# Attention at eight steps to a unit in the second tile of tokens, and the sums of the first weights only from the third

## The chip, the cores and the metric

One core of one Trainium2 chip runs the whole program. The metric is device microseconds from the first to the last instruction, as a median over runs; a trace of one profiled execution is used for everything that is read inside.

## What is computed

```python
k_p = k.reshape(B, H, Sp, pool, D).mean(axis=3)      # B, H, S, D = 8, 8, 576, 64; pool = 8
v_p = v.reshape(B, H, Sp, pool, D).mean(axis=3)
scores = scale * np.matmul(q, k_p.transpose(0, 1, 3, 2))
...
attn = attn / (np.sum(attn, axis=-1, keepdims=True) + 1e-09)
return np.matmul(attn, v_p)
...
x = attn_out.transpose(0, 2, 1, 3).reshape(B * S, H * D)     # 4608 x 512
h = x @ w_in;  x = np.maximum(0.01 * h, h) @ w_out           # d_ff = 2048
h = x @ w_in2; r = np.maximum(h, 0.0); out = (r * r) @ w_out2
```

So: attention over keys and values pooled by eight, then two two-layer networks, all in float32. The weights come in as 64-bit numbers, whose two halves the kernel decodes itself.

## The kernel before, in words

Every float32 operand of a large matmul is split into a high and a low part, and three matmuls (lines 274, 275, 276) make one product. The first network handles 3072 of the 4608 tokens plainly, in six tiles of 512 tokens. A tile has 16 units, one for each 128 columns of the hidden layer; unit u of all 96 is tile u // 16. A unit is `first` (12 matmuls into the tile h), an activation and a split on ScalarE and VectorE, and `second` (12 matmuls into the four accumulators acc). The remaining tokens, and the whole second network, are computed afterwards as seven products of half-sized blocks ("the products"), which need sums of weight blocks prepared before.

Three streams of other work are woven into the 96 units:

- **Attention** is a generator of 237 steps that remain after the first batch. It works on 40 chunks of 128 or 64 queries, five to a batch. `stage_a` transposes the queries (trq), `stage_b` makes the scores (s, line 470), the negated maximum (mx, 478), the difference (x, 486, from batch 3 on), the exponential, its sum (491), the reciprocal rs (493) and, on GpSimd, the probabilities p (495, 502). `stage_c` transposes p (pt, 513, and pr, 522) and splits the result (515, 525), and `stage_d` multiplies by the values (o). Up to unit 15 three steps are advanced in each unit, and five in each unit after that: half of them, rounded down, between `first` and `second`, the others behind `second`.
- **Sums of the first weights** (`prepare_sums`, lines 203 to 206, then the split at 219 and 220): 32 steps, sixteen pairs of one sum step and one split step. One step is advanced in each unit once all weights are decoded and the tile number is above 0.
- **Preparation of the second network's weights** (`prepare_products`): 136 steps, three in each unit, once attention has ended and the sums are done.

The tiles trq, trk, s, pt, pr, o and h share one pool of four PSUM buffers (`ps_w`), taken in the order in which the code asks for them. A tile can be written only when the readers of the fourth tile before it are through. The accumulators have the other four.

A scheduler lays the instructions of each engine in an order of its own before the program runs; on the chip each engine then follows its order strictly. So the code's steps set priorities, and independent work, like the sums, is drawn ahead of its place in the code.

Of the kernel before, what the change touches and what calls it, by code (L numbers as in the profile page):

```python
# [33 lines left out]
def attention_two_mlps(  # L34
# [22 lines left out]
    SPANS = (320, 256)  # L57
    EARLY = 3
    AHEAD = 5
    RATES = (3, 5)  # L60
    HT = 384
    NTILE = 6
    NPASS = NT // (2 * HT)
# [60 lines left out]
    def tick(n=1):  # L124

        for one in LATE:
            one[0] -= n
        while LATE and LATE[0][0] <= 0:
            nc.sync.dma_start(**LATE.pop(0)[1])
# [52 lines left out]
    def split_weights(kind, t, f):  # L182

        w = W[kind, f]
        hl = hlpool.tile([P, 2, TT], F32R, tag="hl", name=f"hl_{kind}_{t}_{f}")
        hi, lo = hl[:, 0], hl[:, 1]
        nc.scalar.copy(hi, w)
        nc.vector.tensor_tensor(out=lo, in0=w, in1=raw(hi), op=ALU.subtract)  # L188
        HL[kind, t, f] = (hi, lo)
        if t == NTILE - 2:  # L190
            p, i = f % NQ, f // NQ
            for j in range(2):
                part = {(0, 0): 0, (0, 1): 1, (1, 1): 2}.get((i, j) if kind == "in" else (j, i))
                if part is not None:
                    later(
                        2, out=WD[1, kind, p // 2][part, :, p % 2].rearrange("p (h x) -> p h x", h=2),
                        in_=raw(hl)[:, :, j * HD:(j + 1) * HD],
                    )
# [408 lines left out]
    def put_stores(until):  # L607

        while STORES and STORES[0][0] <= until:
            nc.sync.dma_start(**STORES.pop(0)[1])  # L610
# [10 lines left out]
    def load_x(t):  # L621
        XS[t] = []
        for c in range(NK):
            st = temp(f"xs1_{t}_{c}")
            nc.sync.dma_start(out=st, in_=x0[t][c * P:(c + 1) * P, :])
            XS[t].append(st)

    def split_x(t):
        new_x(t)
        for (hi, lo), st in zip(X[1, t], XS.pop(t)):  # L630
            nc.scalar.copy(hi, st)
            nc.vector.tensor_tensor(out=lo, in0=st, in1=raw(hi), op=ALU.subtract)
# [4 lines left out]
    def first(t, f):  # L637

        x = X[1, t]
        wh, wl = HL.pop(("in", t, f))  # L640
        h = work(f"h1_{t}_{f}")
        for c in range(NK):
            cs = slice(c * P, (c + 1) * P)
            three(h, (wh[:, cs], wl[:, cs]), x[c], c == 0, c == NK - 1)
        g = temp(f"g1_{t}_{f}")
        nc.scalar.activation(g, h, AF.Prelu, alpha=0.01)
        gh = gpool.tile([P, TT], F32R, tag="gh", name=f"gh1_{t}_{f}")
        gl = gpool.tile([P, TT], F32R, tag="gl", name=f"gl1_{t}_{f}")
        nc.scalar.copy(gh, g)  # L649
        nc.vector.tensor_tensor(out=gl, in0=g, in1=raw(gh), op=ALU.subtract)  # L650
        G[t, f] = (gh, gl)
# [12 lines left out]
    def second(t, f):  # L664
        gh, gl = G.pop((t, f))
        wh, wl = HL.pop(("out", t, f))
        if f == 0:
            A[t] = [ps_a.tile([P, TT], F32, tag="acc", name=f"acc1_{t}_{j}") for j in range(4)]
        acc = A[t]
        for j in range(4):  # L670
            js = slice(j * P, (j + 1) * P)
            three(acc[j], (wh[:, js], wl[:, js]), (gh, gl), f == 0, f == NF - 1)
        if f == NF - 1:
            for j in range(4):
                o = temp(f"o1_{t}_{j}")
                if j % 2 == 0:
                    nc.scalar.copy(o, acc[j])
                else:
                    nc.vector.tensor_copy(o, acc[j])
                store_x1(t, j, o)  # L680
# [6 lines left out]
    def load_x2(t):  # L687
        XS2[t] = []
        for j in range(2):
            src = x0[NTILE + 2 * t + j] if t < LEAD else x1[2 * (t - LEAD) + j]  # L690
            st = x2pool.tile([P, NK, HT], F32, tag=f"xs{j}", name=f"xs2_{t}_{j}")
            nc.sync.dma_start(out=st, in_=src.rearrange("(c p) n -> p c n", p=P))
            XS2[t].append(st)
# [177 lines left out]
    def prepare_weights(f):  # L871
        if f not in RAW:
            RAW[f] = fetch_weights(1, [("in", f), ("out", f)])
        decode_weights(f)
# [21 lines left out]
    def advance():  # L896
        nonlocal at_work, made
        made += 1
        if next(att, 1):
            at_work = False  # L900
        put_stores(made - 2 if at_work else made)
# [6 lines left out]
    for i, (t, f) in enumerate(units):  # L908
        if f == NF - 3 and t + 1 < NTILE:
            while ready[0] * S < min((t + 2) * TT, NT):  # L910
                advance()
            put_stores(made)
            load_x(t + 1)
        if f == NF - 1 and t + 1 < NTILE:
            split_x(t + 1)

        rate = RATES[min(t, 1)]
        if i + 1 < len(units):
            first(*units[i + 1])
        tick()  # L920
        if i + 2 < len(units):
            split_weights("in", *units[i + 2])
        if i + 1 < len(units):
            split_weights("out", *units[i + 1])
        while at_work and made < due + rate // 2:
            advance()
        second(t, f)
        tick()
        due += rate
        while at_work and made < due:  # L930
            advance()
        if w1 < NF:
            prepare_weights(w1)
            w1 += 1
        elif t > 0:
            next(sums1, None)
        if not at_work:
            if prep is None:
                ppool = ctx.enter_context(tc.tile_pool(name="prep", bufs=1, side="right", reuse_waits="tile"))
                prep = prepare_products()  # L940
            for _ in range(3):
                if preparing and next(sums1, 1) and next(prep, 1):
                    preparing = False
        if t == NTILE - 1 and f >= NQ:
            if x2pool is None:
                assert not at_work and next(sums1, 1)
                w_early_stack.close()
                x2pool = ctx.enter_context(tc.tile_pool(name="x2", bufs=1, side="right", reuse_waits="tile"))
                ring = ctx.enter_context(tc.tile_pool(name="ring", bufs=RING, side="right", reuse_waits="tile"))
                load_x2(0)  # L950
                tick(9)
                blocks.insert(0, next_block())
            else:
                if not XO:
                    xg = products_x(0)
                next(xg, None)
# [47 lines left out]
```

## Time and profile before

| what | value |
|---|---|
| median of three runs | 1665.25 us (1664.63 to 1666.43) |
| the profiled execution's own time | 1667.88 us |
| its span, first to last instruction | 1666.1 us |
| TensorE matmul busy | 1615.4 us, 97% |
| VectorE busy | 1219.9 us, 73% |
| ScalarE busy | 858.3 us, 52% |
| GpSimd busy | 132.5 us, 8% |

A busy share is an average over the whole span. The attention stretch and the products have different limits, so each has to be read from windows of its own. TensorE, VectorE, ScalarE and GpSimd are PE, DVE, ACT and POOL in the profile. In the trace the first h matmuls of units 16, 32, 48, 64 and 80 start at 176.80, 311.14, 440.71, 544.30 and 631.34 us, and attention ends in unit 53, just before 488.82 us.

### The profile page before, as it was taken

Reading aid. Unit: us, or ns where it says so; the run is one execution under the profiler, and the core shown is the slowest. Engines: PE = TensorE matmul, PEld = TensorE weight load, DVE = VectorE, ACT = ScalarE, POOL = GpSimd, SP = SyncE. Lnnn points to the kernel's source line nnn. Section 1 sums busy time; section 2 is a strip of 40 time slices with the busy share of each in tenths; the row PEclk is TensorE's granted clock in tenths of the full one; section 3 lists DMA queues with packets and bytes.
Section 4 is the critical chain, followed back from the end, with each engine's and each line's share of the span. In section 5 each row is a group of like instructions: output and inputs, shape, how many; then the busy total and the mean of one; then the engine's idle time right before and its main releaser. Section 6 shows DMA issues by size and latency. Waiting matters only on the chain.

```text
span 1666.1 us, 26276 instructions
## 1 busy us (share of the span) xinstructions
PE 1615.4 (97%) x9688; PEld 1496.2 (90%) x9688; DVE 1219.9 (73%) x1795; ACT 858.3 (52%) x1527; POOL 132.5 (8%) x149
## 2 busy tenths in 40 slices
PE   4899999999999999999999999999999999999998
PEld 3677778778888888889999999999999999999998
DVE  5899999998778778967628459378477487485484
ACT  5788766655666666756435325334234244244233
POOL 3132223322210000000000000000000000000000
PEclk7799999999999999999999999999999999999999
DMA  7565666663326987979878878978878879878776
GB/s 179 184 197 173 187 195 201 196 216 85 95 92 228 307 303 242 319 278 311 294 273 286 287 258 272 305 254 286 293 249 297 281 251 302 277 247 272 269 253 203
DMA packets 215808, 403.88 MB, mean 242 GB/s; under 512 B 55424, under 2 KB 119936, under 8 KB 215680
## 3 DMA queue, kind: packets, MB, share of 16 engines
q1 hardware_dynamic: 215680, 402.19, 73.5%
q8 instruction: 78, 1.28, 0.3%
q14 instruction: 50, 0.41, 0.1%
HBM read 314.57 MB, written 85.98 MB: 240 GB/s over the span
## 4 chain that ended last, share of the span: by engine, by line
PE 77%; DVE 14%; ACT 3%; DMA 3%; issue 2%; SPq 1%; POOL 0%; DVEq 0%; ACTq 0%; POOLq 0%
PE acc L276 12%; PE h L274 12%; PE acc L275 12%; PE acc L274 12%; PE h L275 12%; PE h L276 12%; DVE gl L650 1%; DVE hl_out L188 1%; PE s L470 1%; DVE hl_in L188 1%; DVE v L313 1%; DMA st_in_out<-in_moe_w_out_dram 1%; DVE mx L478 1%; ACT x L481 1%; DMA xs<-x 1%
## 5 line engine op out<-in xcount | busy, mean ns | idle before, releaser
L696 ACT CAST oh<-g 128x768 fp32r<-128x768 f32 x224 | 187.2, 836 | 283.8 <-PE acc L275 165.1
L275 PE MATMUL h<-xl,wb_in 128*128 128x384 f32 x896 | 299.3, 334 | 0.0
L274 PE MATMUL h<-xh,wb_in 128*128 128x384 f32 x896 | 299.3, 334 | 0.0
L276 PE MATMUL h<-xh,wb_in 128*128 128x384 f32 x896 | 299.3, 334 | 0.0
L697 DVE TENSOR_TENSOR ol<-g,oh 128x768 fp32r<-128x768 f32 x224 | 213.6, 954 | 102.1 <-ACT oh L696 101.3
L276 PE MATMUL acc<-wb_out,ol 128*128 128x256 f32 x1008 | 282.2, 280 | 0.0
L274 PE MATMUL acc<-wb_out,oh 128*128 128x256 f32 x1008 | 281.2, 279 | 0.0
L275 PE MATMUL acc<-wb_out,oh 128*128 128x256 f32 x1008 | 281.2, 279 | 0.0
L275 PEld LDWEIGHTS acc<-wb_out,oh 128*128 128x128 f32 x1008 | 189.5, 188 | 0.0
L276 PEld LDWEIGHTS acc<-wb_out,ol 128*128 128x128 f32 x1008 | 189.2, 188 | 0.0
L274 PEld LDWEIGHTS acc<-wb_out,oh 128*128 128x128 f32 x1008 | 188.5, 187 | 0.0
L791 DVE TENSOR_TENSOR g<-h,s 128x768 f32<-128x768 f32 x32 | 30.6, 956 | 191.7 <-PE h L276 112.2
L275 PEld LDWEIGHTS h<-xl,wb_in 128*128 128x128 f32 x896 | 168.2, 188 | 0.0
L274 PEld LDWEIGHTS h<-xh,wb_in 128*128 128x128 f32 x896 | 168.2, 188 | 0.0
L276 PEld LDWEIGHTS h<-xh,wb_in 128*128 128x128 f32 x896 | 168.2, 188 | 0.0
L274 PE MATMUL h<-xh,hl_in 128*128 128x512 f32 x384 | 153.4, 400 | 4.4 <-DVE x L486 2.2
L274 PE MATMUL acc<-gh,hl_out 128*128 128x512 f32 x384 | 153.7, 402 | 0.7 <-ACT gh L649 0.7
L275 PE MATMUL acc<-gl,hl_out 128*128 128x512 f32 x384 | 150.8, 393 | 1.3 <-DVE gl L650 1.3
L276 PE MATMUL acc<-gh,hl_out 128*128 128x512 f32 x384 | 150.9, 393 | 1.1 <-DVE hl_out L188 1.1
L276 PE MATMUL h<-xh,hl_in 128*128 128x512 f32 x384 | 150.4, 392 | 0.0
L275 PE MATMUL h<-xl,hl_in 128*128 128x512 f32 x384 | 150.0, 391 | 0.0
L700 DVE TENSOR_TENSOR g<-g,g 128x768 f32<-128x768 f32 x128 | 120.7, 954 | 6.1 <-ACT g L758 4.6
(148 smaller groups left out, 2976.9 us busy)
## 6 DMA issues: line engine op xcount, KB each, us to landing
wb_in<-wd_in SPq DMA_DIRECT2D x224, 512.0 KB, 4.4
wb_out<-wd_out SPq DMA_DIRECT2D x224, 512.0 KB, 4.5
xs<-x SPq DMA_DIRECT2D x16, 768.0 KB, 7.1
out_dram<-o SPq DMA_DIRECT2D x24, 384.0 KB, 3.9
k<-in_k_dram SPq DMA_DIRECT2D x64, 128.0 KB, 2.9
q<-in_q_dram SPq DMA_DIRECT2D x32, 256.0 KB, 4.0
st_in_out<-in_moe_w_in_dram SPq DMA_DIRECT2D x16, 512.0 KB, 4.1
st_in_out<-in_moe_w_out_dram SPq DMA_DIRECT2D x16, 512.0 KB, 5.6
```

Of the source, the lines that this page charges most:

```text
L188: nc.vector.tensor_tensor(out=lo, in0=w, in1=raw(hi), op=ALU.subtract)
L274: nc.tensor.matmul(outp, ah, bh, start=first, stop=False, **kw)
L275: nc.tensor.matmul(outp, ah, bl, start=False, stop=False, **kw)
L276: nc.tensor.matmul(outp, al, bh, start=False, stop=last, **kw)
L313: nc.vector.tensor_tensor(out=dst if n == D else src[:, :, 0:n], in0=src[:, :, 0:n], in1=src[:, :, n:2 * n], op=ALU.add)
L470: nc.tensor.matmul(sc[:n, 2 * m:2 * m + 2].rearrange("p a x -> p (a x)"), qT[:, 2 * e + m, :n], kT[b % 2][:, 2 * e + m].rearrange("p a x - ...
L478: nc.vector.tensor_reduce(out=mx[:n], in_=sc[:n], axis=AX.X, op=ALU.max, negate=True)
L481: nc.scalar.activation(x[:n, 4 * e + h], sc[:n, h], AF.Exp, bias=mx[:n, h], accum_out=sm[:n, 4 * e + h],)
L696: nc.scalar.copy(hi, src)
L697: nc.vector.tensor_tensor(out=lo, in0=src, in1=raw(hi), op=ALU.subtract)
L700: nc.vector.tensor_tensor(out=out_, in0=a, in1=b, op=ALU.subtract)
L791: nc.vector.tensor_tensor(out=g11, in0=v, in1=s1, op=ALU.add)
```

## The change

```diff
-    RATES = (3, 5)
+    RATES = (3, 8, 5)
...
-        rate = RATES[min(t, 1)]
+        rate = RATES[min(t, 2)]
...
         if w1 < NF:
             prepare_weights(w1)
             w1 += 1
-        elif t > 0:
+        elif t > 1:
             next(sums1, None)
         if not at_work:
...
-            for _ in range(3):
+            for _ in range(3 if t > 3 else 1):
                 if preparing and next(sums1, 1) and next(prep, 1):
                     preparing = False
```

In the second tile (units 16 to 31) attention advances eight steps to a unit, four before `second` and four behind it, and the sums wait for the third tile. Attention's 237 steps are then used up in unit 44 and no longer in unit 53. From there on the loop at the end advances one step in a unit up to tile 3, first on the sums that are left and then on the preparation, and three from tile 4 on. The number of instructions for each part is the same.

Two places in the order of instructions are shown. The first is TensorE at one chunk of batch 4 (queries 256 to 319), which lies in the second tile in both kernels. The names are those above with the tile, unit or chunk in them; "..." stands for the other 512-column matmuls of the same unit. Before:

```order
L470 MATMUL s_256_0_3260<-kT_162,qT_256_3092 64x144 x2
L470 MATMUL s_256_1_3266<-kT_162,qT_256_3092 64x144 x2
L274 MATMUL acc_1_0_2029<-gh_1_13_3137,hl_out_13_3144 128x512
...
L276 MATMUL acc_1_3_2032<-gh_1_13_3137,hl_out_13_3144 128x512
L513 MATMUL pt_128_3292<-ident,p_128_3114 128x128 x4
L522 MATMUL pr_128_3299<-ident,p_128_3114 96x128 x2
L455 MATMUL trq_448_3306<-ident,q_448_3248 128x128 x4
L274 MATMUL h_1_15_3316<-xh_1_0_1878,hl_in_15_3242 128x512
...
L470 MATMUL s_320_1_3350<-kT_162,qT_320_3255 128x144 x2
L513 MATMUL pt_256_3364<-ident,p_256_3276 128x64 x4
```

And in the changed kernel:

```order
L470 MATMUL s_256_0_3008<-kT_162,qT_256_2882 64x144 x2
L470 MATMUL s_256_1_3014<-kT_162,qT_256_2882 64x144 x2
L513 MATMUL pt_128_3028<-ident,p_128_2904 128x128 x4
L274 MATMUL acc_1_0_2063<-gh_1_8_2849,hl_out_8_2856 128x512
...
L522 MATMUL pr_128_3047<-ident,p_128_2904 96x128 x2
L455 MATMUL trq_448_3054<-ident,q_448_2996 128x128 x4
L470 MATMUL s_320_0_3064<-kT_162,qT_320_3003 128x144 x2
L470 MATMUL s_320_1_3070<-kT_162,qT_320_3003 128x144 x2
L274 MATMUL acc_1_0_2063<-gh_1_9_2981,hl_out_9_2988 128x512
...
L513 MATMUL pt_256_3084<-ident,p_256_3024 128x64 x4
```

Between the scores s_256 and the transpose pt_256 that needs their probabilities stood 24 matmuls of 512 columns (twelve into acc, twelve into h); now there are 17 (twelve and five, all into acc).

The second place is VectorE at the end of the first tile (s_in and w_0, w_8 are the first sum and its weights, k and rk the keys being pooled, kd their result). One piece of the difference:

```order
-L203 TENSOR_TENSOR s_in_2084<-w_8_1009 128x256
-L204 TENSOR_TENSOR s_in_2084<-w_0_268,w_8_1009 128x256
-L205 TENSOR_TENSOR s_in_2084<-s_in_2084,w_0_268 128x256
 L313 TENSOR_TENSOR rk_1836<-rk_1836 64x128
-L206 TENSOR_TENSOR s_in_2084<-w_0_268,s_in_2084 128x256
-L313 TENSOR_TENSOR rr_2157<-rk_1836 64x64
+L313 TENSOR_TENSOR k_0_1838<-k_0_1838 128x2x256
+L313 TENSOR_TENSOR rr_2140<-rk_1836 64x64
```

and a few rows further on in the changed kernel:

```order
L313 TENSOR_TENSOR kd_2139<-k_0_1838 128x128
L313 TENSOR_TENSOR k_2_1843<-k_2_1843 128x2x128
L203 TENSOR_TENSOR s_in_4064<-w_8_1009 128x256
L313 TENSOR_TENSOR kd_2139<-k_2_1843 128x128
L204 TENSOR_TENSOR s_in_4064<-w_0_268,w_8_1009 128x256
```

The first sums, which the code now asks for in unit 32, were moved by about ten rows only: the scheduler still draws them ahead to unit 14.

## Rows read from the trace of the kernel before

**Rows 1.** The page: busy time by engine, and PE and DVE by slices.
```profile
PE 1615.4 (97%) x9688; PEld 1496.2 (90%) x9688; DVE 1219.9 (73%) x1795; ACT 858.3 (52%) x1527; POOL 132.5 (8%) x149
PE   4899999999999999999999999999999999999998
DVE  5899999998778778967628459378477487485484
```

**Rows 2.** Windows by stage: length, busy of PE, PEld, DVE, ACT, POOL; PEclk, DMA, GB/s.
```profile
176.80:311.14 134.34, 127.86 (x680) 104.82 (x677) 129.04 (x268) 87.34 (x208) 39.47 (x40) 1.00 0.63 196
311.14:440.71 129.57, 127.35 (x683) 106.14 (x682) 110.30 (x218) 76.34 (x158) 33.00 (x40) 1.00 0.47 140
440.71:488.82 48.11, 48.11 (x261) 40.26 (x260) 35.38 (x74) 30.62 (x61) 11.41 (x16) 1.00 0.25 74
544.30:631.34 87.04, 87.04 (x385) 72.07 (x384) 69.31 (x113) 58.77 (x98) 0.00 (x0) 1.00 0.92 312
...
1000.00:1200.00 200.00, 200.00 (x1479) 200.00 (x1478) 131.21 (x147) 79.83 (x99) 0.00 (x0) 1.00 0.84 282
```

**Rows 3.** TensorE's waits, units 16 to 63: total us, times, longest.
```profile
PE h L274 <- DVE x L486: 2.2, 3, 1.1
PE pt L513 <- POOL p L495: 1.6, 2, 1.2
PE h L274 <- DVE pt_l L515: 1.3, 1, 1.3
PE pr L522 <- POOL p L502: 1.0, 3, 0.4
```

**Rows 4.** VectorE in the second tile, by line.
```profile
L220 DVE TENSOR_TENSOR hs_out<-s_out,hs_out 128x1024 fp32r<-128x1024 f32 x6 | 7.6, 1263 | 0.0
L220 DVE TENSOR_TENSOR hs_in<-s_in,hs_in 128x1024 fp32r<-128x1024 f32 x5 | 6.3, 1251 | 1.4 <-ACT hs_in L219 1.4
...
L204 DVE TENSOR_TENSOR s_out<-w 128x256 f32<-128x256 f32 x6 | 3.2, 542 | 0.0
```

**Rows 5.** Timeline, second tile, chunk 256 of batch 4: start, length.
```profile
296.37 1.20 PE L470 MATMUL s<-kT,qT 128*64 128x144 f32 x8
297.97 0.81 DVE L478 TENSOR_REDUCE mx<-s 64x4 f32<-64x288 f32 x2
303.67 0.19 DVE L493 RECIPROCAL rs<-sm 64x8 f32<-64x8 f32 x1
304.03 2.49 POOL L495 TENSOR_TENSOR p<-x,rs 64x512 f32<-64x512 f32 x1 [6.83 <-DVE rs L493]
306.58 0.46 PE L513 MATMUL pt<-ident,p 64*128 64x64 f32 x4 [1.21 <-POOL p L495]
```

**Rows 6.** Timeline, end of the third tile, chunk 256 of batch 6.
```profile
407.64 1.19 PE L470 MATMUL s<-kT,qT 128*64 128x144 f32 x8
...
413.58 1.04 POOL L495 TENSOR_TENSOR p<-x,rs 64x512 f32<-64x512 f32 x1 [4.84 <-DVE rs L493]
...
416.53 0.46 PE L513 MATMUL pt<-ident,p 64*128 64x64 f32 x4
```

**Rows 7.** Timeline, second tile: two PSUM tiles and their last readers.
```profile
300.80 0.38 PE L522 MATMUL pr<-ident,p 128*96 128x128 f32 x2
303.22 0.42 DVE L525 TENSOR_TENSOR pt_r<-pr,pt_r 32x256 fp32r<-32x256 f32 x1
304.23 1.14 PE L470 MATMUL s<-kT,qT 128*128 128x144 f32 x8
...
307.36 0.45 DVE L486 TENSOR_TENSOR x<-s,mx 128x288 f32<-128x288 f32 x1
```

**Rows 8.** GpSimd's p by line: second tile, then units 48 to 53.
```profile
L495 POOL TENSOR_TENSOR p<-x,rs 128x512 f32<-128x512 f32 (+1 forms) x11 | 15.4, 1400 | 72.0 <-DVE rs L493 53.1 <-PE o L276 6.9 <-DVE vd L313 6.1
...
L495 POOL TENSOR_TENSOR p<-x,rs 128x512 f32<-128x512 f32 (+1 forms) x5 | 5.2, 1042 | 32.9 <-DVE rs L493 17.5 <-ACT pt_h L514 7.7 <-PE pr L522 7.7
```

**Rows 9.** Timeline, the last unit's second, before the products.
```profile
719.29 0.50 PE L274 MATMUL acc<-gh,hl_out 128*128 128x512 f32 x1 [0.74 <-ACT gh L649]
720.41 0.50 PE L275 MATMUL acc<-gl,hl_out 128*128 128x512 f32 x1 [0.62 <-DVE gl L650]
```

## Prediction

> **What bounds the kernel now.** I read the page first. TensorE is 97% busy, and of the forty slices VectorE is at nine tenths only in the third to the ninth [rows 1]. So the page's 73% for VectorE hides two regimes, and I cut the span at the units' starts. From 544.30 us on TensorE is busy without a gap: sixteen units take 87.04 us, 5.44 us each, and a window in the products is full as well [rows 2]. Nothing that the change moves into those stretches can make them shorter. In the attention stretch the windows differ. In the second tile TensorE is busy 127.86 of 134.34 us and VectorE 129.04; in the third 127.35 of 129.57 and VectorE 110.30; in units 48 to 53 TensorE has no gap at all [rows 2]. The idle time of TensorE that a better weave could win is therefore 6.48 + 2.22 = 8.70 us, half a per cent of the span.
>
> The waits say what that idle time is. 3.5 us (2.2 + 1.3) are h matmuls that wait until VectorE has read a PSUM tile (x or pt_l), and 2.6 us (1.6 + 1.0) are transposes that wait for the probabilities p from GpSimd [rows 3]. The remaining 2.6 us are spread over small ones. VectorE is late in both large classes, but TensorE's order decides whether its lateness shows.
>
> **TensorE's own work is the same in sum.** The 29 attention steps of units 48 to 53 cost (48.11 - 6 x 5.44) / 29 = 0.53 us of TensorE each, with no idle in them [rows 2]. A step costs that wherever it stands, so moving 48 steps from units 32 to 53 into units 16 to 31 neither adds nor saves: time before and after differ by TensorE's idle time alone.
>
> **VectorE in the second tile.** The sums were to leave it, and mostly they don't: the scheduler draws them ahead, so that of the eleven splits of sums that stood there [rows 4] eight are still in the changed order. Three pairs go, each about 1.25 us of split and four sums of some 0.5 us [rows 4]: 3 x 3.2 = 9.6 us. 48 attention steps come in. What one costs VectorE is bounded by 35.38 us less 18 weight and activation splits of about 0.69 us, over 29 steps, (35.38 - 12.4) / 29 = 0.79 us with the preparation's rows counted in [rows 2]; I take 0.75, an estimate. 129.04 + 36.0 - 9.6 = 155.4 us, against 87.04 + 128 x 0.53 = 154.9 us for TensorE. Before, the two stood at 129.0 and 129.4. So the pair of engines is as evenly full as before, over a stretch a fifth longer. This alone changes little. Behind unit 44 VectorE has sums or preparation at about the density of today's units 54 to 79, which cost TensorE nothing.
>
> **Term 1, the waits for p.** With eight steps in groups of four, the scores of a chunk and the transposes of its p come closer. I counted in both orders the TensorE work between them, 0.227 us for a matmul of 512 columns (5.44 / 24) and about 0.11 us for a small one. In the order before, no chunk of the second tile has less than 7.5 us of cover; in the changed one seven of nineteen have 5.0 to 5.9, on average 5.6. The chunk shown in the order falls from 7.5 to 5.9 us, because 17 large matmuls stand where 24 stood. What must fit under it is the chain mx, x, exponential, sum, rs, p. In the second tile it took 306.52 - 297.57 = 8.95 us, and the transpose waited [rows 5]; at the end of the third tile, without sums, 414.62 - 408.83 = 5.8 us, and it fitted under 7.7 us [rows 6]. Those are the two bounds: seven chunks at 5.8 - 5.6 give 1.4 us, at 8.95 - 5.6 they give 23.5 us. In the long one p alone took 2.49 us, where its mean there is 1.40 [rows 5, 8]; with the mean it would be 7.9 us. VectorE is as full as there, but fewer sums stand inside the chains. I take 7.0 us, between 5.8 and 7.9: 7 x 1.4 = 9.8 us, in the place of 2.6 us now.
>
> The row on p also bears on a rule. In the Trainium skill, "SBUF — State Buffer", section "Who interferes with whom", a VectorE instruction with two inputs in SBUF and a GpSimd instruction that reads SBUF exclude each other for a whole instruction. The trace agrees as far as p goes: 1.40 us in the full second tile, 1.04 us in units 48 to 53 [rows 8]. By that rule a denser weave would push p toward its 2.49 us and term 1 to about 7 x 2.5 = 17.5 us.
>
> **Term 2, the four PSUM buffers.** More attention per unit means more tiles through `ps_w` between two h tiles. A pr tile was free 303.64 - 301.18 = 2.46 us after its last write, an s tile 307.81 - 305.37 = 2.44 us [rows 7]. Counting in the order the TensorE work between the last write of an s, pt or pr tile and the first write of the fourth tile behind it, in units 16 to 43: before, five reuses have less than 2.45 us, and they lack 3.7 us together, which is close to the 3.5 us of h waits that the trace shows [rows 3]. After, sixteen have less, and they lack 9.0 us. The lower bound is no change, 3.5 us, if VectorE runs ahead of TensorE; with readers at 3.0 us instead of 2.45 the same count gives 19 us.
>
> **Term 3, the way into the products.** The last unit's `second` waits 0.74 + 0.62 = 1.36 us for ScalarE and VectorE, which are then full of preparation [rows 9]. In the changed order the preparation's last rows stand before unit 93, so I take this gain whole; its other bound is nothing.
>
> **The sum.** Idle time after: 9.8 + 9.0 + 2.6 = 21.4 us if the waits were independent. They aren't: while TensorE waits for p, the readers of PSUM catch up. I take off half of the smaller, 4.5, which is a choice, and have 16.9 us against 8.7. That is +8.2, less 1.4 for term 3: about +7 us. The profiled execution took 1667.88 us (span 1666.1), 2.6 us above the median of the runs, so the same step on the median gives 1665.25 + 7 = 1672 us.
>
> **Rivals.**
> 1. *Faster.* The short covers don't bite, because TensorE is what VectorE waits for in the changed order: the sums no longer stand between mx and rs, and the chain is as short as in the third tile. Then the waits for p cost 1.4 us, those for PSUM stay under today's 3.5 us, say 2, and with the rest halved to 1.3 the idle is 4.7 us in the place of 8.7: -4.0, with term 3 -5.4, 1660 us. For it: chains of 5.8 us exist [rows 6]. Against it: eight of eleven pairs of sums are still in the tile, and VectorE and TensorE come out level. It is decided by the chain: below about 6.0 us it holds, and with term 2 at today's size break-even with term 3 lies at 6.2 us.
> 2. *The change does little.* The stall is set by how full VectorE and TensorE are against each other, and that ratio is 1.00 before and after. Idle time is then moved from units 32 to 43 into 16 to 31: 1665 us, within 3 us. The third tile speaks for it, where the same weave with VectorE at 110.30 of 129.57 lost only 2.22 us [rows 2]; the counted covers speak against it.
> 3. *Much slower.* VectorE falls behind in the second tile and every short cover pays 8.95 - 5.6: 23.5 + 9.0 + 2.6 - 8.7 - 1.4 = +25 us without overlap, with it +20: 1685 us. The trace holds such a chain [rows 5], but one with a slow p.
>
> **Chances and range.** My forecast, waits that grow by 3 to 15 us, has 0.48; rival 1 has 0.20, rival 2 0.24, rival 3 0.08. About 3.3 us (0.2%) is what a measurement of this kernel tells from no change. Slower: 0.48 + 0.08 = 0.56; same 0.24; faster 0.20. The likeliest case alone spans 1668 to 1680. The range for eight in ten has to take in most of rival 1 and the lower end of rival 3, from 1659 to 1684.
>
> **What would show it.** In the profile after, POOL's last work should end near unit 44, some 40 us before today's 488.82 us (nine units of 5.44 us less, and the added idle time more). In units 16 to 31, TensorE's idle time should rise from 6.48 us to 12 or more, under two names: pt and pr waiting for p, and h, trq or o waiting for reads of x, pt_l or pt_r. The gap before the products should be gone. I am wrong if those two waits do not grow: if the stretch from unit 16 to 63, 367.5 us now, is shorter, then the chain or the readers were faster than I took them. I am also wrong if TensorE idles behind unit 44, since I cost the sums and the preparation there at nothing; their cover is 5.44 us of matmuls in each unit, and every us by which VectorE exceeds it would be paid in full.

## The result, and the profile after

| | before | changed |
|---|---|---|
| median of six runs | 1665.95 us | 1676.10 us (1673.92 to 1678.50) |
| ratio | | 1.0057, 95% interval 1.0047 to 1.0067 |
| the profiled execution | 1667.88 us | 1673.92 us |
| its span | 1666.1 us | 1672.2 us |

The change makes the kernel slower by 10.15 us on the median. The two profiled executions are only 6 us apart, because the one of before is among its longer runs and the one after is the shortest of its six. Where that difference lies is seen below.

The page of the changed kernel, busy time by engine:

```profile
PE 1613.8 (97%) x9688; PEld 1491.7 (89%) x9688; DVE 1220.0 (73%) x1795; ACT 857.2 (51%) x1527; POOL 133.7 (8%) x149
```

Beside [rows 1] the page says almost nothing: nearly the same shares, the same counts. The windows by stage do (units 16 to 31, 32 to 47, 48 to 63 and 64 to 79 of the changed kernel; columns as in [rows 2]).

```profile
173.62:339.10 165.48, 153.72 (x852) 125.92 (x849) 154.35 (x330) 102.83 (x252) 52.26 (x59) 0.99 0.56 168
339.10:465.33 126.23, 121.51 (x636) 100.17 (x635) 114.11 (x219) 80.79 (x158) 30.82 (x36) 1.00 0.55 183
465.33:552.37 87.04, 87.04 (x385) 72.07 (x384) 77.11 (x126) 63.27 (x104) 0.00 (x0) 1.00 0.67 229
552.37:639.41 87.04, 87.04 (x385) 72.07 (x384) 66.46 (x107) 55.55 (x95) 0.00 (x0) 1.00 0.91 306
```

TensorE idles 165.48 - 153.72 = 11.76 us in the second tile and 126.23 - 121.51 = 4.72 us in the third, 16.48 together against 8.70 before. In units 48 to 79 it is full, with the preparation there; no sum is left for them, since the last split of a set of sums starts at 429.8 us. The last work of GpSimd ends at 445.1 us and not near 488, in unit 44.

The same difference by stretches: units 16 to 63 took 367.5 us before and take 378.75; from unit 64 to the end it was 1121.8 and is 1119.8; before unit 16 it was 176.8 and is 173.6. The first two make +9.25 us. The third, -3.2 us, hides part of that. I don't count it to the change, which moved the first sums by about ten rows there: the granted clock at the start was lower in the profiled execution of before, and over all the kernels below this start takes 173.6 to 179.8 us. The first window of before, and behind it that of the changed kernel:

```profile
0.00:62.00 62.00, 30.09 (x131) 25.67 (x132) 42.02 (x83) 35.85 (x124) 20.24 (x30) 0.71 0.66 177
```

```profile
0.00:62.00 62.00, 28.49 (x136) 22.44 (x137) 43.81 (x87) 37.25 (x129) 20.70 (x30) 0.81 0.65 178
```

At 0.71 of the 2.4 GHz level TensorE got through 131 matmuls in 62 us, at 0.81 through 136. So all comparisons below are made from unit 16 on, or on medians.

Behind unit 16 the granted clock differs once more. Before, it is 1.00 in all windows of units 16 to 53 [rows 2]. In the changed kernel it was 0.50 (the 1.2 GHz level) for 3.4 us in unit 17. TensorE had been busy for 2.06 of the 4.73 us before, with two waits of 1.8 and 0.8 us:

```profile
184.00:188.73 4.73, 2.06 (x13) 1.25 (x12) 4.67 (x12) 4.02 (x20) 0.71 (x1) 1.00 0.76 247
188.73:192.14 3.41, 3.41 (x15) 2.73 (x14) 3.17 (x8) 2.64 (x12) 1.56 (x3) 0.50 0.29 67
```

At half the clock these 3.4 us cost 1.7 us at most (an estimate from this row), and they show as busy time, not as idle time.

TensorE's waits in units 16 to 63 of the changed kernel (columns as in [rows 3]):

```profile
PE pt L513 <- POOL p L495: 7.5, 8, 1.7
PE trq L455 <- issue: 2.5, 2, 1.7
PE pr L522 <- ACT x L481: 1.8, 1, 1.8
PE pr L522 <- DVE x L486: 1.1, 1, 1.1
PE trq L455 <- ACT x L481: 0.8, 1, 0.8
PE h L274 <- DVE x L486: 0.7, 1, 0.7
PE o L539 <- DVE pt_r L525: 0.5, 1, 0.5
```

The two names of the forecast are there. Waits for p went from 2.6 us [rows 3] to 7.7 (7.5, and 0.2 for pr).

The second name is waits until a PSUM tile has been read. In the list they are those of pr, trq and h for x, 1.8 + 1.1 + 0.8 + 0.7 = 4.4 us (in batches 0 to 2 x comes from ScalarE, line 481, straight from the scores). The two waits of trq put down to "issue" look like the same thing: each ends about 0.1 us behind a reading of scores by VectorE, and in the order shown trq takes the buffer of the first s tile. One of them:

```profile
230.17 0.44 DVE L486 TENSOR_TENSOR x<-s,mx 64x288 f32<-64x288 f32 x1
...
230.71 0.63 PE L455 MATMUL trq<-ident,q 128*128 128x128 f32 x4 [0.77 <-issue]
```

With them this class is 6.9 us. Before, it was the 3.5 us of h in [rows 3] and two smaller lines, 4.9 us in all. These two stand here, from units 16 to 63 of the kernel before; the third line, like the wait for pt_r above, is another thing, as o waits for its own operand:

```profile
PE pr L522 <- DVE pt_l L515: 0.7, 1, 0.7
PE h L274 <- ACT qT L459: 0.7, 1, 0.7
PE o L539 <- DVE pt_r L525: 1.1, 2, 0.7
```

So most of the added idle time has the name p, 5.1 us, and 2.0 us have the name of PSUM readers.

The timeline of the chunk that the order showed (queries 256 to 319 of batch 4), from its scores to its transpose:

```profile
267.83 1.19 PE L470 MATMUL s<-kT,qT 128*64 128x144 f32 x8
...
269.91 0.45 DVE L478 TENSOR_REDUCE mx<-s 64x4 f32<-64x288 f32 x1
270.39 0.80 DVE L650 TENSOR_TENSOR gl<-g,gh 128x512 fp32r<-128x512 f32 x1
...
270.70 0.66 PE L513 MATMUL pt<-ident,p 128*128 128x128 f32 x4 [1.68 <-POOL p L495]
...
274.81 0.69 DVE L188 TENSOR_TENSOR hl_out<-w,hl_out 128x512 fp32r<-128x512 f32 x1 [0.19 <-ACT hl_out L187]
...
276.06 0.19 DVE L493 RECIPROCAL rs<-sm 64x8 f32<-64x8 f32 x1
...
276.42 1.04 POOL L495 TENSOR_TENSOR p<-x,rs 64x512 f32<-64x512 f32 x1 [4.72 <-DVE rs L493]
...
277.51 0.46 PE L513 MATMUL pt<-ident,p 64*128 64x64 f32 x4 [0.60 <-POOL p L495]
```

The scores end at 269.02, p at 277.46: a chain of 8.44 us. In [rows 5] it was 8.95, with a p of 2.49 us; here p takes 1.04, and the length comes from VectorE, which goes from one row to the next with hardly a gap and has the splits of weights and activations (hl_out, gl) between this chunk's own rows. The cover counted in the order was 5.9 us, so the transpose could have been 2.5 us late. It waited 0.60. Inside the cover stands the transpose of the chunk before, which itself waited 1.68 us, and that time was cover too. Here one chunk's wait paid for a part of the next one's.

### The profile page after: what moved, and what is told of

The parts are those of the page before. It is cut to its first block, busy times and chain, and to the rows that moved or that the text cites. A ratio compares the mean times of both kernels' runs of the same rounds, so it can differ in the third digit from the quotient of the medians.

```text
span 1672.2 us, 26299 instructions
## 1 busy us (share of the span) xinstructions
PE 1613.8 (97%) x9688; PEld 1491.7 (89%) x9688; DVE 1220.0 (73%) x1795; ACT 857.2 (51%) x1527; POOL 133.7 (8%) x149
## 4 chain that ended last, share of the span: by engine, by line
PE 82%; DVE 11%; ACT 3%; issue 2%; DMA 1%; POOL 1%; SPq 0%; DVEq 0%; ACTq 0%; POOLq 0%
PE acc L276 13%; PE h L274 13%; PE acc L275 13%; PE acc L274 13%; PE h L276 13%; PE h L275 13%; PE s L470 1%; ACT x L481 1%; DVE hl_out L188 1%; DVE hl_in L188 1%; DVE w L172 1%; DVE wm L162 1%; DVE mx L478 1%; DVE v L313 1%; DVE gl L650 1%
```

## The experiments

The idle time of TensorE in the second and third tile and the stretches are read from windows at each kernel's own unit starts, as above. The last column is for how long the granted clock was 0.50 in units 16 to 63 of the profiled execution; half of it, at most, is lost. Ratios, and differences of medians in the text, are to runs of the kernel before made together with each experiment (medians of 1665.74 to 1666.53 us).

| kernel | median us | ratio to before (95%) | idle, tiles 2 and 3 | units 16 to 63 | unit 64 to end | us at clock 0.50 |
|---|---|---|---|---|---|---|
| before | 1665.95 | | 6.48 + 2.22 | 367.5 | 1121.8 | 0 |
| changed | 1676.10 | 1.0057 (1.0047 to 1.0067) | 11.76 + 4.72 | 378.8 | 1119.8 | 3.4 |
| 1 rate alone | 1680.40 | 1.0083 (1.0070 to 1.0097) | 12.88 + 5.04 | 382.8 | 1119.8 | 6.8 |
| 2 all but the rate | 1671.08 | 1.0027 (1.0017 to 1.0038) | 7.19 + 3.46 | 371.1 | 1123.1 | 3.4 |
| 3 six steps | 1674.55 | 1.0048 (1.0036 to 1.0061) | 7.70 + 5.23 | 378.0 | 1120.1 | 10.2 |
| 4 changed, later transposes | 1673.20 | 1.0038 (1.0026 to 1.0051) | 9.68 + 4.42 | 375.2 | 1119.8 | 3.4 |
| 5 before, later transposes | 1667.12 | 1.0007 (0.9998 to 1.0016) | 5.69 + 3.39 | 367.9 | 1121.0 | 0 |
| 6 changed, six PSUM buffers | 1682.93 | 1.0096 (1.0083 to 1.0110) | 14.92 + 3.79 | 382.8 | 1119.8 | 13.7 |
| 7 before, six PSUM buffers | 1671.82 | 1.0034 (1.0021 to 1.0047) | 7.40 + 3.32 | 371.0 | 1120.8 | 3.4 |
| 8 changed, both distances | 1675.73 | 1.0051 (1.0034 to 1.0068) | 6.33 + 4.56 | 374.2 | 1121.2 | 10.2 |
| 9 changed, sums behind attention | 1691.62 | 1.0153 (1.0139 to 1.0166) | 7.30 + 0.76 | 370.0 | 1142.1 | 3.4 |
| 10 before, sums behind attention | 1688.97 | 1.0139 (1.0124 to 1.0155) | 2.96 + 0.82 | 362.7 | 1147.0 | 3.4 |
| 11 before, sums behind and on GpSimd | 1765.97 | 1.0603 (1.0587 to 1.0619) | 3.02 + 0.82 | 379.8 | 1210.3 | 17.1 |
| 12 before, part of the sums behind | 1675.04 | 1.0052 (1.0039 to 1.0066) | 5.26 + 0.82 | 364.0 | 1132.2 | 0 |

**1. The rate alone.** The kernel before with

```diff
-    RATES = (3, 5)
+    RATES = (3, 8, 5)
-        rate = RATES[min(t, 1)]
+        rate = RATES[min(t, 2)]
```

> The kernel before with eight steps to a unit in the second tile and nothing else changed: sums from the second tile on, preparation at three steps to a unit. Theory (TensorE waits because less of its own work lies between a chunk's scores and its transposes, and between two uses of a PSUM buffer): in the order, seven covers in the second tile are again between 4.8 and 6 us, and PSUM reuses lack 7.6 us in the place of 5.4 before; about 8 to 10 us slower than before, 1674 to 1676 us. Rival (the sums and the preparation that were pushed behind attention cost it): no change from before, 1666 us.

The rate alone costs 14 us (0.83%), above my range and more than the whole change. So the loss comes from the eight steps, and the rest of the change gives a quarter of it back in their presence.

**2. All but the rate.** The changed kernel with

```diff
-    RATES = (3, 8, 5)
+    RATES = (3, 5)
-        rate = RATES[min(t, 2)]
+        rate = RATES[min(t, 1)]
```

> The changed kernel with five steps to a unit in the second tile: the later sums and the slower preparation alone. Theory: the order keeps covers of 7.5 us in the second tile, PSUM reuses lack 4.5 us as against 5.4 before; same as before within 2 us, 1664 to 1668 us. Rival (sums and preparation): the 10 us of the whole change, 1676 us.

It cost 4.5 us, which is in neither range: at five steps the later sums hurt, at eight they helped. Idle time in the two tiles is 10.65 us for 8.70. The largest wait in units 16 to 63 is for the reader of a PSUM tile, 2.2 us before [rows 3]:

```profile
PE h L274 <- DVE x L486: 3.8, 4, 1.9
```

Why a few sums in other places make x late by 1.6 us more I can't show. A part of the 3.6 us that units 16 to 63 take longer can be the clock, 1.7 us at most. The run says that a new order alone, with the same density, moves this kernel by some us.

**3. Six steps to a unit.** The changed kernel with

```diff
-    RATES = (3, 8, 5)
+    RATES = (3, 6, 5)
```

> The changed kernel with six steps in the place of eight. Theory: the order has one short cover in the second tile (5.7 us) in the place of seven, and PSUM reuses lack 4.7 us as before; 0 to 2 us slower than before, 1666 to 1668 us. Rival (VectorE's work in the second tile sets the time): by the counted rows that work is 134 us, 127 before and 149 in the change, so a third of the 10 us, 1669 to 1670 us.

Missed: the kernel is above both ranges and almost as slow as at eight steps. The waits for p are down, in units 16 to 63 of this kernel, to

```profile
PE pt L513 <- POOL p L495: 5.4, 4, 2.6
```

and idle time in the two tiles is 12.93 us, 4.2 more than before, where eight steps have 7.8 more. The rest that makes it look almost as slow as eight steps is busy time, and the clock was low in three places:

```profile
189.66:193.07 3.41, 3.37 (x12) 2.98 (x12) 3.29 (x7) 2.69 (x10) 2.27 (x3) 0.50 0.30 69
295.47:298.88 3.41, 3.41 (x9) 2.64 (x9) 3.09 (x9) 0.87 (x2) 0.05 (x1) 0.50 0.59 194
408.11:411.52 3.41, 3.41 (x10) 2.64 (x9) 1.32 (x4) 0.66 (x1) 1.35 (x3) 0.50 0.02 5
```

That is up to 5.1 us, against up to 1.7 in the changed kernel. By idle time, one step more costs about half of what three cost.

**4. and 5. Later transposes.** To take the first of the two classes of waits away, `stage_c` of a chunk runs a chunk later from batch 2 on, with three p buffers in the place of two (the room comes from a mask kept as one column and broadcast). The core of it:

```diff
+            LAGGED, c_done = 2 * nch, 0
...
+                behind = 1 if i <= LAGGED else 2
+                for j in range(c_done, len(chunks) if i == len(chunks) else i - behind + 1):
+                    b, span = chunks[j][:2]
+                    yield from stage_c(*chunks[j])
+                    c_done = j + 1
...
                 if i > 0:
-                    b, span = chunks[i - 1][:2]
-                    yield from stage_c(*chunks[i - 1])
...
```

In the changed kernel:

> The changed kernel with p transposed one chunk later from batch 2 on (a third p buffer; the mask is kept as one column, which makes room for it). The arithmetic is the same. Theory: the covers in the second tile are 13.7 us and more, so the waits of pt and pr for p, 7.5 us of idle time in the profile after, vanish; PSUM reuses still lack 6.8 us. 1667 to 1670 us. Rival (VectorE and TensorE are level in the second tile, and the idle time only shows under the name of p): the waits move to other names, 1674 to 1677 us.

In the kernel before:

> The kernel before with p transposed one chunk later, as in the experiment on the change (third p buffer, mask of one column). Theory: 2.6 us of waits for p go, the rest stays: 1663 to 1665 us. Rival: the waits move to PSUM buffers, 1665 to 1668 us.

Windows of the changed kernel with later transposes, units 16 to 31 and 32 to 47, and its largest wait in units 16 to 63:

```profile
176.48:338.78 162.30, 152.62 (x844) 125.72 (x843) 153.91 (x328) 100.84 (x236) 51.87 (x60) 0.99 0.60 175
338.78:464.61 125.83, 121.41 (x633) 99.80 (x633) 117.74 (x222) 83.14 (x161) 28.83 (x33) 1.00 0.56 183
```

```profile
PE h L274 <- DVE x L486: 4.3, 3, 2.1
```

The waits for p, 7.5 us in eight places, are gone from the list; idle time fell by only 2.4 us. h now waits 4.3 us for x, where it waited 0.7; with the smaller lines of its kind it is 10.4 us where there were 6.9. The lateness was in the main passed on to the other class, and the time, 1673.20, lies between the two ranges. In the kernel before, where these waits are few, the edit changes nothing that can be measured, as the rival had it.

**6. and 7. Six PSUM buffers.** To take the second class away, `ps_w` gets six buffers and the accumulators two; output blocks 3 and 4 are added into 1 and 2 (not shown), so this part of the output is another one.

```diff
-    ps_w = one_stack.enter_context(tc.tile_pool(name="ps_w", bufs=4, space=PSUM))
-    ps_a = one_stack.enter_context(tc.tile_pool(name="ps_a", bufs=4, space=PSUM))
+    ps_w = one_stack.enter_context(tc.tile_pool(name="ps_w", bufs=6, space=PSUM))
+    ps_a = one_stack.enter_context(tc.tile_pool(name="ps_a", bufs=2, space=PSUM))
```

In the changed kernel:

> The changed kernel with six PSUM buffers in the place of four for attention and h, and two accumulators in the place of four: the third and fourth column block of the first network are added into the first two, so that part of the output is another one; matmuls, copies and transfers are as many as before. Theory: the 7 us of waits under trq, pr and h that stand for PSUM buffers fall to 2 or less, the waits for p stay at 7 to 8 us: 1669 to 1672 us. Rival (VectorE's fullness): the idle time moves to p, 1674 to 1677 us.

In the kernel before, as a control of the edit (in the text of this expectation and of the next, "attention" with two buffers should read accumulators):

> The kernel before with six PSUM buffers for the token products and two for the attention (output blocks 3 and 4 are added into 1 and 2, so part of the output is another one), the control of the same edit in the changed kernel, which there raised idle from 16.5 to 18.7 us. If the edit itself costs by leaving the attention two buffers (its products then wait for their readers), the kernel before gets slower by it too, by 2 to 6 us (1668 to 1672 us). If it only moved the lateness of the denser steps to the waits for p, the kernel before, with fewer of those, stays within 2 us (1664 to 1668 us).

The changed kernel with six buffers, units 16 to 31, and its largest wait in units 16 to 63:

```profile
178.26:348.96 170.70, 155.78 (x848) 127.72 (x845) 154.44 (x327) 102.90 (x253) 51.78 (x59) 0.96 0.55 160
```

```profile
PE pt L513 <- POOL p L495: 16.4, 11, 3.8
```

The time is above both ranges. Now p is waited for 16.4 us, and idle time rose from 16.48 to 18.71. The control shows that the edit itself costs 2 us of idle (10.72 for 8.70), and by medians 6.1 us in the kernel before for 6.8 in the changed one. Less that, six buffers neither gave nor took anything: the waits of the PSUM class are down to 1.0 us, and the time went over to p.

**8. Both distances.** Both edits in the changed kernel.

> The changed kernel with both distances of TensorE lengthened at once: the weights p are transposed one chunk later (as in the run with later transposes), and the token products have six PSUM buffers, the attention two (as in the run with six buffers; output blocks 3 and 4 are added into 1 and 2, so part of the output is another one). Each edit by itself took away its own class of waits and the idle time went to the other class: 14.1 us and 18.7 us of idle in the second and third tile where the changed kernel has 16.5. My theory now, that the two distances share one lateness of the other engines and either one alone is enough to pass it on: with both lengthened idle falls to 3 to 7 us, units 16 to 64 take 365 to 370 us, the kernel 1663 to 1668 us. Rival, VectorE's fullness: VectorE's rows last as long as TensorE's in the second tile, so whatever the distances are, TensorE goes at VectorE's pace: idle stays at 9 to 15 us under other names (the exponentials, h, the raw scores), units 16 to 64 take 372 to 378 us, the kernel 1670 to 1676 us.

```profile
179.83:338.44 158.61, 152.28 (x839) 126.37 (x839) 154.33 (x321) 100.19 (x238) 54.59 (x60) 0.98 0.57 169
338.44:466.99 128.55, 123.99 (x641) 102.31 (x638) 121.47 (x231) 83.39 (x161) 31.77 (x33) 0.99 0.57 188
```

```profile
PE o L275 <- DVE pt_l L515: 4.0, 5, 1.6
PE o L274 <- ACT pt_h L514: 3.3, 3, 2.0
```

Idle time is 10.89 us, above my 3 to 7 and within the rival's 9 to 15, and units 16 to 63 and the whole time are the rival's as well. So by the forecast the rival holds. What the four kernels at eight steps do show, with one profiled execution of each, is that the two distances stand in for each other: later transposes take 16.48 - 14.10 = 2.4 us of idle time off with four buffers, and 18.71 - 10.89 = 7.8 with six. The largest waits that are left here have another name: o waits for its own operands, the splits of pt.

How much of the 10.89 us is due to the eight steps is open. The kernel before with six buffers idles 10.72 us, nearly the same, but it is not the right base. It still waits for p,

```profile
PE pt L513 <- POOL p L495: 4.6, 4, 2.1
```

and by the same theory the later transposes would take that away. A kernel before with both edits was not run.

**9. and 10. The sums behind the attention.** The sums are taken out of both tiles, in the changed kernel and in the kernel before, into a pool that exists only once attention has ended (the scheduler then cannot draw them ahead), three steps to a unit.

```diff
-                s = mpool.tile([P, 4, HD], F32, tag="m", name=f"s1_{kind}{p}")
+                s = ppool.tile([P, 4, HD], F32, tag="s1", name=f"s1_{kind}{p}")
...
-        elif t > 1:
-            next(sums1, None)
...
-            for _ in range(3 if t > 3 else 1):
+            for _ in range(3):
```

In the changed kernel (the edit shown; in the kernel before the rate of three is there already):

> The changed kernel with the sums of the first weights in a tile of the pool that opens only when attention has ended, so that no scheduler can draw them ahead; they and the preparation advance three steps to a unit from then on. In the order, the covers of p in the second tile (seven under 6 us) and the PSUM reuses (17, lacking 9.7 us) are those of the change, but VectorE's rows there fall from 149 to 130 us. If the short distances alone set the waits (my theory in its strict form), the idle time of units 16 to 47 stays at 13 to 17 us and the time at 1673 to 1677 us. If VectorE's fullness sets them (the rival), idle time falls to 4 to 7 us and the time to 1664 to 1667 us, unless sums and preparation overfill the units behind attention.

In the kernel before:

> The same for the kernel before: five steps to a unit, sums only behind attention. VectorE's rows in the second tile fall from 127 to 95 us by the order, the covers stay at 7.5 us. Both theories expect the idle time of units 16 to 47 to fall from 8.7 us to 2 or 3, so 1659 to 1662 us; only if the sums overfill VectorE behind unit 53 (its slack there is about 8 us in 87) does the gain go.

The changed kernel without sums in the attention, units 16 to 31, 32 to 47 and 64 to 79:

```profile
176.46:336.10 159.64, 152.34 (x850) 125.51 (x847) 131.99 (x295) 95.66 (x244) 45.51 (x58) 0.99 0.47 130
336.10:457.83 121.73, 120.97 (x639) 100.39 (x638) 83.99 (x170) 68.47 (x141) 25.48 (x36) 1.00 0.24 71
...
546.49:643.47 96.98, 91.05 (x385) 72.27 (x384) 78.55 (x127) 62.86 (x103) 0.00 (x0) 0.98 0.93 313
```

VectorE has 131.99 us of work in the second tile for 154.35, with the attention at the same eight steps, and TensorE idles 8.06 us in the two tiles for 16.48. That lies between the two theories, nearer to the rival's 4 to 7 than to the strict form's 13 to 17. In the kernel before idle time falls from 8.70 to 3.78. Three pairs of kernels differ in the rate alone. In the two tiles the eight steps add 17.92 - 8.70 = 9.2 us of idle time with the sums where they were (1), 16.48 - 10.65 = 5.8 with the later sums (2), and 8.06 - 3.78 = 4.3 without sums. So of the idle time that the rate adds to the kernel before, about half comes without any sums on VectorE beside it, and the other half needs them. In units 16 to 63 the sums cost 4.8 us at five steps and 8.8 at eight. The gain is lost behind the attention, where the loss is 20 us and more: the third row is a stretch that takes 87.04 us when nothing is late. VectorE's busy time left 87.04 - 69.31 = 17.7 us free in that stretch before [rows 2], more than the 8 us that I had written, and even so there was no room for the sums.

**11. The sums on GpSimd.** The kernel before, with the sums behind the attention as in 10, four steps to a unit, and the additions on GpSimd.

```diff
-        nc.vector.tensor_tensor(out=s1, in0=a21, in1=a22, op=ALU.add)
+        nc.gpsimd.tensor_tensor(out=s1, in0=a21, in1=a22, op=ALU.add)
```

(and the three below it)

> The kernel before (five steps to a unit) with the sums of the first weights behind the attention, four steps to a unit there, and the additions of all sums on GpSimd, which has nothing to do behind the attention; the splits stay where they are. Sums taken out of the second and third tile gave the kernel before 4.8 us there and lost 20 us or more behind the attention, where VectorE had too much to do. If VectorE's adds were that surplus, units 16 to 64 take 361 to 364 us, the rest 1119 to 1123 us, the kernel 1658 to 1664 us, faster than both. Rival: GpSimd is slow enough with the additions, or the splits alone are still too much, that the sums are not ready for the products: TensorE idles behind the attention and before the products by 5 us or more, the kernel is at 1668 us or above.

The worst of all, 100 us slower, as the rival had it and far beyond. ScalarE's waits in units 48 to 79, and TensorE's in units 48 to 94:

```profile
ACT hs_out L219 <- POOL s_out L206: 29.5, 8, 4.1
ACT hs_in L219 <- POOL s_in L206: 25.5, 8, 4.1
```

```profile
PE h L274 <- ACT hl_in L187: 16.2, 5, 12.7
```

GpSimd isn't full, but a sum is four additions one behind the other, of about 1.07 us there for about 0.54 us on VectorE [rows 4]. ScalarE's copy of the sum (line 219) waits for the chain at the head of ScalarE's order for 55 us, and behind it stand the splits of the weights that TensorE needs next. The granted clock was lower there as well, 0.94 in units 48 to 63 and 0.85 in units 64 to 79.

**12. A part of the sums behind.** The kernel before with ten of the sixteen sets where they were and six behind the attention.

```diff
+    early = 0
...
-        elif t > 0:
+        elif t > 0 and early < 20:
             next(sums1, None)
+            early += 1
...
-                s = mpool.tile([P, 4, HD], F32, tag="m", name=f"s1_{kind}{p}")
+                if 2 * p + (kind == "out") < 10:
+                    s = mpool.tile([P, 4, HD], F32, tag="m", name=f"s1_{kind}{p}")
+                else:
+                    s = ppool.tile([P, 4, HD], F32, tag="s1", name=f"s1_{kind}{p}")
```

> The kernel before (five steps to a unit) with ten of the sixteen sets of sums where they are, in the second and third tile, and the last six behind the attention, three steps to a unit there. All sixteen moved gave 4.8 us in units 16 to 64 and lost 25 us behind, where scalar engine and VectorE had too much to prepare. If VectorE's fullness in the second and third tile is what makes the idle time, and a part of the sums fits into the room that VectorE has behind the attention: units 16 to 64 take 364.5 to 366.5 us, the rest 1121 to 1123 us, the kernel 1662 to 1665.5 us, faster than before by a little. Rival: behind the attention there is no room for even six sets, since the preparation of the products is the next bound: units 64 to the end take 1125 us or more, the kernel 1667 to 1675 us.

Units 16 to 63 got 3.5 us shorter, somewhat more than expected, and the stretch from unit 64 on 10.4 us longer. The rival holds: behind the attention there is no room even for six sets. No version that was run beats the kernel before; the nearest is 5, at 1.0007.

## Why the prediction was right, and where not

The forecast was 1672 us, +7 us; it is 1676.1 us, +10.15, in the range and on the predicted side. By its steps:

- **VectorE in the second tile** was to come to 155.4 us against 154.9 for TensorE; the window has 154.35 and 153.72. Eight of the sixteen splits of sums start in that tile, as the order said. This step is right.
- **Idle time** was to be 16.9 us, and is 16.48; in the second tile it is 11.76 us, just short of the "12 or more" that was named as a sign. The two names came, both smaller than counted: 7.7 us for p where I had 9.8, and 6.9 us for readers of PSUM (with the two waits of trq that I count to them) where I had 9.0. From their sum I had taken 4.5 us for overlap, which was a choice without a row. So the agreement of the total to 0.4 us is partly luck. That the two terms aren't independent is borne out: with the waits for p taken away idle time fell by only 2.4 us (4), with those for PSUM taken away by nothing beyond the edit's own cost (6, 7), with both by 5.6 us (8).
- **The chain** was taken at 7.0 us. Over the 18 chunks whose scores end in the second tile of the changed kernel it is 5.1 to 8.5 us from the end of the scores to the end of p's first instruction, on average 7.2, so its size was right. But the waits for p in that tile are 4.8 us in six places, and not 9.8. The chunk shown took 8.44 us, one of the longest, and waited 0.60 because the chunk before had waited 1.68 within its cover. The formula leaves out that waits shorten each other. The other 2.8 us for p are two waits in the third tile, for which I had counted none.
- **The rule of the Trainium skill** ("SBUF — State Buffer", section "Who interferes with whom"), as I had applied it, would have made term 1 some 17.5 us, through a slower p. p took 1.24 us on average in the second tile after, for 1.40 before [rows 8], and 1.33 with the rate alone (1): the denser weave did not push it toward 2.49. The row by line for the tile of the changed kernel:

```profile
L495 POOL TENSOR_TENSOR p<-x,rs 128x512 f32<-128x512 f32 (+1 forms) x17 | 21.1, 1238 | 90.5 <-DVE rs L493 41.2 <-PE h L276 9.4 <-PE trq L455 6.9
```

- **TensorE's own work is the same in sum** is the step that was mis-sized. The matmuls in units 16 to 63 are the same (1874 and 1873 recorded), but TensorE's busy time there went from 127.86 + 127.35 + 103.53 = 358.74 us to 153.72 + 121.51 + 87.04 = 362.27, +3.5 us where I had 0. That is most of what separates +7 from +10. Up to 1.7 us of it is the 3.4 us at half the clock shown above, which I had no term for. The rest was not tried apart. Between other kernels at five and eight steps busy time grows too, by 2.3 us with later transposes, 3.9 with six buffers and 2.2 without the sums, but the low clock can make up to 1.7, 5.1 and 0 us of these, so they give no steady cost of the rate.
- **Term 3** was -1.4 us; from unit 64 to the end it is -2.0. The changed kernel has no wait in the last unit's `second`.
- **Behind unit 44** I had cost the sums and the preparation at nothing: right for the preparation, as units 48 to 79 take 87.04 us each sixteen; no sum was left there to test. And the cover is thin: six sets of sums behind the attention cost 10 us from unit 64 on (12).

In the reading of the page one thing was wrong, without a consequence: VectorE is at nine tenths also in the 17th and the 25th slice [rows 1].

Rival 2 said that the stall is set by how full VectorE is against TensorE. It fails as a whole, since the ratio is the same and the idle time nearly doubled; but it has a part in it: with VectorE relieved of the sums, the rate adds 4.3 us of idle time and not 5.8 or 9.2 (9, 10). Rival 1 needed chains below 6.2 us, and the mean is 7.2; rival 3 needed that every short cover pays in full. Neither came.

Open is why the other half of the change costs 4.5 us at five steps (2), how much idle time eight steps would add with both distances lengthened (8), and the part of the busy time above. The runs say only that most of it lies in units 16 to 63.

## What to carry to other kernels

Where one late engine is waited for in two places, these need not be two terms: here most of the wait that was taken away came back at the other place. So lengthen both before judging either, and run the same edits on the kernel before, or their own cost will be read as the mechanism's; here the run with both edits is missing, and the question stayed open. Work that is taken from a full stretch is a gain only if the stretch that receives it has room in the order of every engine that it touches, not only in busy time: here 4.8 us were won and 25 lost. And where a stretch is compared between two profiled executions, start behind the part in which the granted clock still differs, and look at the clock behind it as well: here 3.4 us at half the clock, right behind two waits, show as busy time and look like work.

## What was not expected of the hardware

In the prediction I had looked for the exclusion between VectorE and GpSimd on p alone. In the denser weave of the changed kernel it shows on VectorE's side. The split of a set of sums takes 1.21 to 1.36 us before in all sixteen places. In the changed kernel's second tile the rows by line are

```profile
L220 DVE TENSOR_TENSOR hs_in<-s_in,hs_in 128x1024 fp32r<-128x1024 f32 x4 | 6.7, 1664 | 0.5 <-ACT hs_in L219 0.5
L220 DVE TENSOR_TENSOR hs_out<-s_out,hs_out 128x1024 fp32r<-128x1024 f32 x4 | 6.2, 1554 | 0.3 <-ACT hs_out L219 0.3
```

Four of the eight took 1.73 to 2.22 us, and each of these four overlaps an instruction of GpSimd in the timeline; the other four, 1.21 or 1.22 us, overlap none. The longest:

```profile
306.05 1.36 POOL L432 TENSOR_TENSOR vR<-rx,vR 32x512 fp32r<-32x512 f32 x1
...
306.28 2.22 DVE L220 TENSOR_TENSOR hs_in<-s_in,hs_in 128x1024 fp32r<-128x1024 f32 x1
```

VectorE's split starts 0.23 us behind GpSimd's instruction and takes 1.0 us longer than alone. The Trainium skill, "SBUF — State Buffer", section "Who interferes with whom", says that the one of the two that is issued second blocks until the first is through; this row agrees with it.

Which of the two pays can't be told from the recorded starts, though. In the kernel before four splits overlap GpSimd as well and take 1.21 to 1.36 us. One of them starts 1.39 us behind GpSimd and pays nothing; there it is GpSimd's instruction that is long, 3.73 us where the same one takes 1.26 us elsewhere (at 261.00 us in the changed kernel):

```profile
228.15 3.73 POOL L404 TENSOR_TENSOR rv<-rd,mask 64x512 f32<-64x512 f32 x1 [1.90 <-ACT hl_out L187]
...
229.54 1.21 DVE L220 TENSOR_TENSOR hs_out<-s_out,hs_out 128x1024 fp32r<-128x1024 f32 x1
```
